# Causal attention and a cosine MoE in one kernel: tail scores of two pairs together, one transpose for both tails, P V a step later

## The chip, the cores and the metric

The kernel runs on one core of one Trainium2 chip. The metric is device time in microseconds, the median of several runs. The clock that TensorE (PE) was granted stood at 1.00 of its full 2.4 GHz in every stage of the profiled execution.

## What is computed

```python
scores = (1 / sqrt(64)) * q @ k^T          # 4 batches, 12 heads, 448 tokens, head size 64
scores = where(causal mask, -1e9, scores)
attn   = softmax(scores)
x      = (attn @ v) with the heads side by side          # 1792 x 768
h      = x @ w_in                                        # w_in 768 x 2048
out    = (h * cos(h)) @ w_out                            # w_out 2048 x 768
```

Everything is float32.

## The kernel before, in words

The program has an attention stage and a MoE stage. All of it is written out by hand: inside `tc.manual_schedule()` each engine runs its instructions in the order in which the code issues them, so the place of a line in `attention` (L219) is its place in the queue of PE, DVE (VectorE), ACT (ScalarE), POOL (GpSimd) or SP (the queue of loads and stores).

**Attention.** A *pair* is two heads of one batch; there are 24. The 448 tokens are three blocks of 128 and a *tail* of 64. Step `i` of the loop starts pair `i` and carries on with pairs `i-1` to `i-3`:

- PE forms the scores of pair `i`: blocks of 128 rows in `scores_main` (L349, L354; first the *top* block of 384 columns for both heads, then the *low* blocks of 128 and 256), and the tail's 64 rows for both heads in `scores_tail` (L361, L364). Head 0 lies on partitions 0 to 63 of the operands and head 1 on 64 to 127, so that the two heads' products use different rows of the array. In the tail the outputs lie on different partitions of one PSUM bank too.
- PE turns Q and K of pair `i+1`: three blocks each (L319) and one 64-row tail each (L326).
- ACT copies both to SBUF (`evac_qk`, L336 and L338).
- DVE adds the mask, negates and takes the row minimum (`masked`, L372); ACT takes the exponential and the row sum (`exp`, L386); DVE inverts the sums (L397, L398); POOL multiplies (`normalise`, L404).
- PE turns the weights of pair `i-1`: twelve blocks (`tp_blocks`, L426) and the tail as four (`tp_tail`, L436). DVE copies two of the four banks out (L555, L557) and ACT two (L564, L566).
- PE multiplies by V for pair `i-2` (`av`, L450). ACT and DVE write the result as a high and a low part (L466, L470) in the next step.

PSUM has eight banks. `new_bank` hands out 0 to 3 in turn and `score_bank` 4 to 7: the scores of step `i` go into the banks that the turned weights of step `i-1` left.

After each step half of a weight piece is converted (`convert_weight`, L126): even halves take two DVE operations (L134, L137) and a square on ACT (L140), odd halves two DVE operations (L143, L147), a copy on ACT (L148) and a subtraction on POOL (L149). There are twelve pieces, so 24 steps have one half each.

After the last pair, two steps have 18 matmuls of the first MoE product each in front of the turned weights (`fill`, L476).

**MoE.** Slots of two token blocks by eight feature groups (`slot`, L875) follow, and then a stage with fewer products for the remaining tokens (from L1027 on). Only slot `k == 3` is touched, by the order in which its DVE, ACT and POOL work is issued: `c1` are the cosine's stages (L593 to L600), `pb` the packing of a raw weight (L168, L172, L176), `halve` its split into high and low (L702, L703), `m2a_chunk` the products L681 and their sum on DVE (L669).

Of the kernel before, what the change touches and what calls it, by code (L numbers as in the profile page):

```python
# [21 lines left out]
def kernel(  # L22
# [68 lines left out]
    def new_bank():  # L91
        return banks8[:, bank("p", 0, 1, 2, 3)]

    packed = banks8[:, 2:4, 0:EH]

    def score_bank():
        return banks8[:, bank("s", 4, 5, 6, 7)]
# [28 lines left out]
    def convert_weight(st, w, pool, parts=1, j=0, halves=(0, 1)):  # L126
# [4 lines left out]
        if 0 in halves:  # L131
# [8 lines left out]
            nc.scalar.activation(hif, hif, AF.Square)  # L140
        if 1 in halves:
# [6 lines left out]
            nc.scalar.copy(wh, tf)  # L148
# [70 lines left out]
    def attention(filler):  # L219
        with (  # L220
# [3 lines left out]
            rows = f32(land.rearrange("p a e u -> p (a e u)")).rearrange(  # L224
                "p (t c d) -> p t c d", c=NB + 1, d=P
            )
            qn_t = [rows[:, i] for i in range(3)]
            kn_t = [rows[:, 3 + i] for i in range(3)]
            vn_t = [cst.tile([P, NB + 1, P], F32, name=f"vn{i}") for i in range(4)]
# [3 lines left out]
            nat, qkt, prob, ptr = {}, {}, {}, {}  # L233
# [4 lines left out]
            def load_main(dst, src, b, h0, eng=nc.sync):  # L238
                for j in range(2):
                    eng.dma_start(  # L240
                        out=dst[:, 0:NB, heads(j)],
                        in_=src[b, h0 + j, 0 : NB * P, :].rearrange("(c p) d -> p c d", p=P),
                    )

            def load_tail(dst, src, b, h0, eng=nc.sync, p=0):
                eng.dma_start(
                    out=dst[p : p + TAIL, NB, :].rearrange("p (h d) -> p h d", h=2),
                    in_=src[b, h0 : h0 + 2, NB * P : S, :].rearrange("h p d -> p h d"),
                )

            def load_qk(i, keng=nc.sync):
                b, hp = pairs[i]
                qn = qn_t[i % 3]
                kn = kn_t[i % 3]
                load_main(qn, q, b, 2 * hp)
                load_main(kn, k, b, 2 * hp, keng)
                load_tail(qn, q, b, 2 * hp)
                load_tail(qn, k, b, 2 * hp, keng, TAIL)
                nat[i] = [qn, kn]
# [3 lines left out]

            for i in range(3):
                if i == 0:
                    load_qk(0, nc.scalar)

                    nc.scalar.copy(cst.tile([P, 32], BF16, name="tab")[:, 0:1], warm[:, 0:1])
                elif i == 1:
                    load_qk(1, nc.scalar)  # L270
            wps = new_bank()

            def keep_warm(n):
                for _ in range(n):
                    nc.tensor.matmul(wps[:, 0:P], lhsT=warm, rhs=warm, start=True, stop=True)
# [1139 lines left out]
```

## Time and profile before

| | us |
|---|---|
| median of 3 runs (632.76 to 634.29) | 632.78 |
| the profiled execution | 632.72 |
| its span | 630.9 |
| attention, steps 0 to 2 | 17.98 |
| attention, steps 3 to 22 | 143.73 |
| attention, step 23 to the start of the MoE slots | 20.82 |
| PE busy | 622.0 (99%) |
| DVE, ACT, POOL busy | 485.8, 431.5, 438.5 |

A row of the chain names the work that the end of the program waited for at each moment. A timeline row gives start, duration, engine, line, operation and shapes, and in brackets the idle time before it with what ended it. PE's float32 products stand as two records each, one for each pass, and operations that run at once on different rows or columns of the array overlap. Between operations of one engine the difference of two starts says what one costs; a duration includes the tail that the next one overlaps. `128x448` is partitions by columns.

### The profile page before, as it was taken

The page shows a single profiled execution, that of the slowest core. Times are in us where ns is not written, and L with a number is a line of the kernel's source. Part 1 is how long each engine was busy: PE and PEld are TensorE (multiplying, and loading weights), DVE is VectorE, ACT ScalarE, POOL GpSimd, SP SyncE. Part 2 cuts the span into 40 slices and gives each one's busy share as a digit, 9 for nine tenths or more (in the row PEclk, how much of TensorE's full clock was granted, in tenths as well). Part 3 has the DMA queues.
Part 4 walks back from the last instruction along what each step waited for, and adds up shares of the span by engine and source line. Part 5 has one row for each costly group of instructions (what it writes and reads, how often), then busy time and mean ns, then how long its engine had stood idle before and what let it go on. Part 6 is the DMA issues. An engine that isn't in the chain of part 4 may idle for free.

```text
span 630.9 us, 11559 instructions
## 1 busy us (share of the span) xinstructions
PE 622.0 (99%) x3753; PEld 536.2 (85%) x3753; DVE 485.8 (77%) x1072; ACT 431.5 (68%) x953; POOL 438.5 (69%) x432
## 2 busy tenths in 40 slices
PE   9999999999999999999999999999999999999996
PEld 6666666666679998899999999999999999999996
DVE  6988888888847778877777777774358877887887
ACT  5998999999877677877787777753346545644640
POOL 3656656566534868887877778781578789788886
PEclk9999999999999999999999999999999999999999
DMA  6656546456403676969796969769997477559204
GB/s 148 153 133 164 132 114 157 114 139 175 126 10 118 226 280 225 352 223 325 228 341 199 337 224 313 250 235 360 400 403 279 151 258 253 178 170 316 86 2 150
DMA packets 124620, 133.28 MB, mean 211 GB/s; under 512 B 72688, under 2 KB 108896, under 8 KB 124560
## 3 DMA queue, kind: packets, MB, share of 16 engines
q1 hardware_dynamic: 116944, 106.23, 53.2%
q0 software_dynamic: 4928, 24.78, 10.6%
q10 hardware_dynamic: 2688, 1.54, 0.8%
q8 instruction: 30, 0.49, 0.3%
q14 instruction: 30, 0.25, 0.1%
HBM read 82.58 MB, written 49.94 MB: 210 GB/s over the span
## 4 chain that ended last, share of the span: by engine, by line
PE 91%; DVE 4%; ACT 2%; issue 1%; POOL 1%; DVEq 0%
PE banks L681 18%; PE banks L1103 12%; PE banks L1123 12%; PE banks L450 7%; PE banks L585 6%; PE banks L586 6%; PE banks L587 6%; PE banks L354 5%; PE banks L426 5%; PE banks L319 4%; PE banks L364 3%; PE banks L1027 2%; PE banks L1140 2%; PE banks L436 2%; PE banks L326 1%
## 5 line engine op out<-in xcount | busy, mean ns | idle before, releaser
L669 DVE TENSOR_TENSOR acc<-acc,banks 128x768 f32<-128x768 f32 (+1 forms) x122 | 112.7, 932 | 43.8 <-PE banks L681 33.5
L681 PE MATMUL banks<-w,gh 128*128 128x384 f32 x512 | 109.7, 335 | 1.6 <-DVE acc L669 1.6
L404 POOL TENSOR_TENSOR pb<-pb,stat 128x768 f32<-128x768 f32 (+2 forms) x72 | 74.0, 1042 | 50.4 <-ACT pb L386 35.4
L681 PEld LDWEIGHTS banks<-w,gh 128*128 128x128 f32 x512 | 90.8, 188 | 3.2 <-DVE acc L669 2.0
L386 ACT ACTIVATE pb<-pb,stat 128x384 f32<-128x384 f32 (+1 forms) x144 | 71.9, 504 | 9.4 <-DVE stat L372 9.4
L585 PE MATMUL banks<-xa,w 128*128 128x512 f32 x192 | 75.1, 391 | 0.0
L587 PE MATMUL banks<-xa,w 128*128 128x512 f32 x192 | 75.0, 391 | 0.0
L586 PE MATMUL banks<-xa,w 128*128 128x512 f32 x192 | 75.0, 391 | 0.0
L372 DVE CUSTOM_DVE_ANT_0 pb<-banks,mask 128x384 f32<-128x384 f32 (+1 forms) x144 | 53.2, 419 | 17.2 <-PE banks L354 9.2
L681 PE MATMUL banks<-w,gl 128*128 128x384 f32 x256 | 65.1, 335 | 0.0
L703 POOL TENSOR_TENSOR w<-ct,w 128x768 fp32r<-128x768 f32 x28 | 52.0, 1857 | 17.7 <-ACT w L702 12.5
L593 ACT ACTIVATE ni<-banks 128x512 int32<-128x512 f32 (+1 forms) x64 | 34.5, 539 | 33.9 <-PE banks L587 20.0
L612 POOL TENSOR_TENSOR gl<-r,gh 128x512 fp32r<-128x512 f32 x32 | 41.6, 1301 | 19.4 <-ACT gh L611 19.2
L595 DVE SCALAR_TENSOR_TENSOR r<-ni,banks 128x512 f32<-128x512 int32 (+1 forms) x56 | 35.1, 626 | 20.2 <-ACT ni L593 16.9
L597 ACT ACTIVATE r<-r 128x512 f32<-128x512 f32 (+1 forms) x56 | 32.8, 586 | 23.3 <-DVE r L595 22.8
L450 PE MATMUL banks<-pm,vn 128*64 128x448 f32 (+3 forms) x384 | 46.8, 386 | 0.0
L681 PEld LDWEIGHTS banks<-w,gl 128*128 128x128 f32 x256 | 46.4, 188 | 0.0
L1103 PE MATMUL banks<-xb,bb 128*128 128x384 f32 x234 | 44.7, 334 | 0.0
L600 DVE SCALAR_TENSOR_TENSOR r<-r,banks 128x512 f32<-128x512 f32 (+1 forms) x56 | 35.1, 626 | 12.2 <-ACT r L598 12.2
L450 PEld LDWEIGHTS banks<-pm,vn 128*64 128x64 f32 x384 | 25.4, 136 | 22.3 <-issue 15.4
L1123 PE MATMUL banks<-big,gh 128*128 128x384 f32 x168 | 42.6, 334 | 0.0
L587 PEld LDWEIGHTS banks<-xa,w 128*128 128x128 f32 x192 | 36.0, 188 | 7.6
(151 smaller groups left out, 1559.1 us busy)
## 6 DMA issues: line engine op xcount, KB each, us to landing
bb<-w_in_d SPq DMA_DIRECT2D x48, 384.0 KB, 5.4
land<-in_moe_w_in_dram SPq DMA_DIRECT2D x14, 768.0 KB, 5.3
land<-in_moe_w_out_dram SPq DMA_DIRECT2D x14, 768.0 KB, 5.5
w_out_d<-w POOLq DMA_DIRECT2D x14, 768.0 KB, 5.2
big<-w_out_d SPq DMA_DIRECT2D x25, 384.0 KB, 5.2
w_in_d<-w POOLq DMA_DIRECT2D x7, 768.0 KB, 3.9
raw_d<-ct POOLq DMA_DIRECT2D x14, 384.0 KB, 7.2
land<-in_q_dram SPq DMA_DIRECT2D x48, 96.0 KB, 2.8
```

Of the source, the lines that this page charges most:

```text
L372: nc.vector.tensor_tensor_reduce(out=dst, in0=src, in1=m, scale=-1.0, scalar=3.0e38, op0=ALU.add, op1=ALU.min, accum_out=st[:, 0, n : n + 1],)
L386: nc.scalar.activation(dst, dst, AF.Exp, scale=-1.0, bias=st[:, 0, n : n + 1], accum_out=st[:, 1, n : n + 1],)
L404: nc.gpsimd.tensor_tensor(dst, dst, r.to_broadcast(list(dst.shape)), op=ALU.mult)
L450: nc.tensor.matmul(o[heads(j), kc * P : S], lhsT=vn[:, kc, heads(j)], rhs=pm[:, kc, j, kc * P : S], start=(kc == 0), stop=(kc == NB),)
L585: yield nc.tensor.matmul(hv, lhsT=wh[:, f], rhs=x[:, 0, cc, t], start=(cc == 0), stop=False)
L586: yield nc.tensor.matmul(hv, lhsT=wh[:, f], rhs=x[:, 1, cc, t], start=False, stop=False)
L587: yield nc.tensor.matmul(hv, lhsT=wl[:, f], rhs=x[:, 0, cc, t], start=False, stop=(cc == NCC - 1))
L669: nc.vector.tensor_tensor(d, d, o, op=ALU.subtract)
L681: nc.tensor.matmul(o[:, e, 0:EH], lhsT=a[:, cs], rhs=w[:, e * EH : (e + 1) * EH], start=(x == 0), stop=(x == 5),)
L703: nc.gpsimd.tensor_tensor(w[:, 1], tf, f32(w[:, 0]), op=ALU.subtract)
L1103: nc.tensor.matmul(o, lhsT=w[:, u, k * P : (k + 1) * P], rhs=x[k][:, v], start=k + m == 0, stop=k == K - 1 and m == 2,)
L1123: nc.tensor.matmul(o[:, b % 2, 0:EH], lhsT=g_ops[i][u][:, c * P : (c + 1) * P], rhs=wouts[g, i][:, v], start=(x == 0), stop=(x == 2),)
```

## The change

1. **Tail scores.** `scores_tail` goes. In odd steps `scores_ends(i - 1)` forms the tails of pairs `i-1` and `i` together: 384 key columns for two pairs and two heads (four products of 64 rows by 64 columns of the array), then the last 64 key columns for the four. The odd pair's heads are swapped on the output side (`j ^ p % 2`), which puts the four on the four quarters of the array, and the two pairs have a bank each (2 and 3).
2. **One transpose for both tails.** The tails of Q and K are loaded one above the other and turned by one 128x128 transpose (`transpose_ends`) into 128 columns behind Q. Tails of two pairs are loaded by one transfer. Q is copied out as 512 columns and K as 384, without the factor 1/8, which goes into `masked`.
3. **A step later.** The tail's mask, exponential, normalising and transposes trail by a step, P V is for pair `i-3`, and `pm` has three buffers. The loop has one step more, V is loaded a step later, and the filler is cut 14, 12, 10 instead of 18, 18.
4. **Banks by hand.** 0 is P V's, 1 takes Q and later K of the next pair, 4 to 7 the scores and then the turned weights; K's transposes move behind those of the weights.
5. **Weights.** The square (L140) and the copy (L148) go from ACT to POOL.
6. **MoE slot 3.** `pb` and `halve` are issued ahead of the last stages of `c1`.

```diff
-            nc.scalar.activation(hif, hif, AF.Square)
+            nc.gpsimd.tensor_tensor(hif, hif, hif, op=ALU.mult)
...
+            nc.gpsimd.tensor_copy(wh, tf)
             nc.gpsimd.tensor_tensor(wl, tf, f32(wh), op=ALU.subtract)
...
+            def transpose_main(i, which, b):
+                t = qkt[i, which] = flat[:, 2 * which + i % 2], banks8[:, b]
                 for c in range(NB):
+                    nc.tensor.transpose(t[1][:, c * P : (c + 1) * P], nat[i][which][:, c, :], ident)
+
+            def transpose_ends(i, b):
+                nc.tensor.transpose(banks8[:, b, W : W + P], nat[i][2], ident)
...
+            def scores_ends(i):
+
+                for r, w in ((0, W), (W, P // 2)):
+                    for p in (i, i + 1):
+                        qt, kt = qkt[p, 0][0], qkt[p, 1][0]
+                        for j in range(2):
+                            nc.tensor.matmul(
+                                banks8[heads(j ^ p % 2), (TA_BANK, TB_BANK)[p % 2], r : r + w],
+                                lhsT=qt[heads(j), W:S],
+                                rhs=(kt[heads(j), 0:W] if r == 0 else qt[heads(j), S : S + P // 2]),
+                                start=(r == 0), stop=(r != 0),
+                            )
...
-                    out=dst, in0=src, in1=m, scale=-1.0, scalar=3.0e38,
+                    out=dst, in0=src, in1=m, scale=-scale, scalar=3.0e38,
...
-                ptr[i] = at.tile([P, 2 * JUMP], F32, tag="pm", bufs=2, name="pm")
+                ptr[i] = at.tile([P, 2, LEN], F32, tag="pm", bufs=3, name="pm")
...
             def fill(n):
-                for _ in zip(range(n), filler):
+                if not extra:
+                    spare = itertools.cycle((QK, 6))
+                    extra.append(filler_of(lambda: banks8[:, next(spare)]))
+                for _ in zip(range(n), extra[0]):
                     pass
...
+            for i in range(N + 4):
                 cur, prev, nxt = i < N, 0 < i <= N, i + 1 < N
-                old, done = 0 <= i - 2 < N, 0 <= i - 3 < N
+                ends_of, old, done = 0 <= i - 2 < N, 0 <= i - 3 < N, 0 <= i - 4 < N
+                tb = (4, (TA_BANK, 6)[i % 2], 5, (6, 7)[i % 2])
...
-                    load_v(i)
+                if prev:
+                    load_v(i - 1)
...
                 if cur:
                     open_scores(i)
-                    pb, pl, st = prob[i]
-                    top = scores_main(i, TOP)
-                    low = scores_main(i, LOW)
...
-                    tail = scores_tail(i)
-                if nxt and i:
-                    transpose_qk(i + 1, 0)
-                    transpose_tails(i + 1)
-                    transpose_qk(i + 1, 1)
+                    scores_main(i, TOP, SC[0:2])
+                    scores_main(i, LOW, SC[2:4])
+                    if i % 2:
+                        scores_ends(i - 1)
...
+                elif nxt:
+                    transpose_main(i + 1, 0, QK)
+                    transpose_ends(i + 1, QK)
                 if done:
-                    finish_hi(i - 3, av_of[i - 3])
+                    finish_hi(i - 4)
...
+                if 0 < i <= N + 1:
+                    inverse(i - 1, 0 if prev else TAIL_COL, TAIL_COL + (i > 1))
...
-                    inverse(i - 1, LO)
                     normalise_block(i - 1, 0)
                     normalise_block(i - 1, 1)
...
-                if prev:
-                    inverse(i - 1, TL)
-                    normalise(prob[i - 1][1][:, 0:S], prob[i - 1][2], TL)
+                if ends_of:
+                    normalise_ends(i - 2)
...
                         exp_block(i, 2, j)
+                        if i and nxt and j == i % 2:
+                            evac_qk(i + 1, 0, n=W + P)
...
-                    finish_lo(i - 3, av_of.pop(i - 3))
+                    finish_lo(i - 4)
...
+                    inverse(i, TOP_COL, TOP_COL + 2)
+                    normalise_block(i, 2)
+                    masked_block(i, 0, 1, 0, SC[3])
+                    masked_block(i, 1, 1, P, SC[3])
+                    exp_block(i, 0, 0)
+                    exp_block(i, 1, 0)
+                if prev:
+                    masked_ends(i - 1)
+                if i in (N, N + 1):
+                    fill((14, 12)[i - N])
+                if prev:
+                    open_ptr(i - 1)
+                    tp_top(i - 1, tb[0])
+                    tp_first(i - 1, tb[1])
+                if prev:
+                    tp_last(i - 1, tb[2])
                 if nxt and i:
-                    evac_qk(i + 1, 0)
+                    transpose_main(i + 1, 1, QK)
                     evac_qk(i + 1, 1)
                 if cur:
...
+                    exp_block(i, 0, 1)
+                    exp_block(i, 1, 1)
...
+                    exp_ends(i - 1)
+                if ends_of:
+                    tp_ends(i - 2, tb[3])
+                    evac_ends(i - 2, tb[3])
+                if i == N + 2:
+                    run(extra[0])
                 if old:
-                    av_of[i - 2] = av(i - 2)
-                if i == N + 1:
-                    run(filler)
+                    av(i - 3)
...
-                    some(c1)
-                    some(pb)
-                    some(c1)
-                    m2a_chunk(*prev, 1)
-                    run(pb)
-                    tb = halve(ib)
+                    if k == 2:
+                        some(c1)
+                        some(pb)
+                        some(c1)
+                        m2a_chunk(*prev, 1)
+                        run(pb)
+                        tb = halve(ib)
+                    else:
+                        run(pb)
+                        m2a_chunk(*prev, 1)
+                        tb = halve(ib)
+                        some(c1, 2)
```

The order on PE, where a step is what lies between two groups of scores (`pb`, `pl`: the weights' main part and tail; `pm`: turned; `land`: Q and K as loaded). A step before:

```order
L354 MATMUL banks<-flat 128x384 x2
L354 MATMUL banks<-flat 128x128 x2
L354 MATMUL banks<-flat 128x256 x2
L364 MATMUL banks<-flat 64x448 x2
L319 MATMUL banks<-ident,land 128x128 x3
L326 MATMUL banks<-ident,land 128x64 x2
L319 MATMUL banks<-ident,land 128x128 x3
L426 MATMUL banks<-ident,pb 128x128 x12
L436 MATMUL banks<-ident,pl_92 128x128 x4
L450 MATMUL banks<-pm,vn_89 64x448 x2
```

And an odd step of the change; an even one is the same without the two rows of L348:

```order
L336 MATMUL banks<-flat 128x384 x2
L336 MATMUL banks<-flat 128x128 x2
L336 MATMUL banks<-flat 128x256 x2
L348 MATMUL banks<-flat 64x384 x4
L348 MATMUL banks<-flat 64x64 x4
L304 MATMUL banks<-ident,land 128x128 x3
L307 MATMUL banks<-ident,land 128x128
L422 MATMUL banks<-ident,pb 128x128 x12
L304 MATMUL banks<-ident,land 128x128 x3
L442 MATMUL banks<-ident,pl_95 128x128 x4
L457 MATMUL banks<-pm,vn_88 64x448 x2
```

The 23 transposes of a step now stand in one row, and the tail's products come in every second step.

ACT in the same place, an even step of the change (L376 is `exp`, L313 any copy out of PSUM, L475 the high part of P V):

```order
L475 CAST xa<-banks 128x448
L376 ACTIVATE pb,stat<-pb,stat 128x384
L313 COPY flat<-banks 128x512
L376 ACTIVATE pb,stat<-pb,stat 128x384
L376 ACTIVATE pb,stat<-pb,stat 128x128
L376 ACTIVATE pb,stat<-pb,stat 128x256
L313 COPY pm<-banks 128x2x2x128
L313 COPY flat<-banks 128x384
L376 ACTIVATE pb,stat<-pb,stat 128x128
L376 ACTIVATE pb,stat<-pb,stat 128x256
L376 ACTIVATE pl_95,stat<-pl_95,stat 128x448
L313 COPY pm<-banks 128x4x2x64
```

Before, the last copy out of the turned weights stood ahead of three exponentials; now it is the last of the step, and no weight work stands in the queue.

POOL across an odd and an even step of the change (L396 is `normalise`, L134 the square, L142 the copy, L143 the subtraction):

```order
L134 TENSOR_TENSOR st<-st 128x256
L396 TENSOR_TENSOR pb<-pb,stat 128x2x128
L396 TENSOR_TENSOR pb<-pb,stat 128x2x256
L396 TENSOR_TENSOR pl_94<-pl_94,stat 128x448
L396 TENSOR_TENSOR pb<-pb,stat 128x2x384
L142 CAST w_287<-ct 128x256
L143 TENSOR_TENSOR w_287<-ct,w_287 128x256
L396 TENSOR_TENSOR pb<-pb,stat 128x2x128
```

The square and the copy now stand ahead of the next step's first two multiplications.

## Rows read from the trace of the kernel before

**Rows 1.** page, part 1: busy time of each engine over the whole span.

```profile
PE 622.0 (99%) x3753; PEld 536.2 (85%) x3753; DVE 485.8 (77%) x1072; ACT 431.5 (68%) x953; POOL 438.5 (69%) x432
```

**Rows 2.** busy time by stage; columns: window, us, PE, PEld, DVE, ACT, POOL, PEclk, DMA, GB/s.

```profile
6.72:24.70 17.98, 17.26 (x124) 10.83 (x124) 16.42 (x66) 15.68 (x53) 9.41 (x9) 1.00 0.63 148
24.70:168.43 143.73, 143.73 (x1122) 93.37 (x1122) 125.63 (x506) 131.03 (x407) 86.77 (x90) 1.00 0.56 137
168.43:189.25 20.82, 20.52 (x133) 14.40 (x133) 11.13 (x37) 16.08 (x36) 8.08 (x10) 1.00 0.21 62
```

**Rows 3.** chain that ended last, one step; columns: start us, us, what.

```profile
60.63 1.50 PE banks L354 x12
62.13 0.90 PE banks L364 x4
63.03 0.48 PE banks L319 x3
63.51 0.21 PE banks L326 x2
63.71 0.48 PE banks L319 x3
64.19 1.31 PE banks L426 x12
65.50 0.44 PE banks L436 x4
65.94 1.88 PE banks L450 x16
```

**Rows 4.** tail products by line L364, window 54.8:55.0, then 53.3:60.8; min/median/max ns.

```profile
L364 PE MATMUL banks<-flat x2: 587/587/587, 54.9 to 54.9; 64*64 64x448 f32 x2
...
L364 PE MATMUL banks<-flat x4: 536/562/587, 54.9 to 55.3; 64*64 64x448 f32 x4
```

**Rows 5.** timeline of ACT, the step from 60.63; columns: start us, us, instruction.

```profile
62.27 0.61 ACT L386 ACTIVATE pb<-pb,stat 128x384 f32<-128x384 f32 x1 [0.48 <-DVE stat L372]
...
64.67 0.39 ACT L386 ACTIVATE pb<-pb,stat 128x128 f32<-128x128 f32 x1
...
65.05 0.39 ACT L386 ACTIVATE pb<-pb,stat 128x128 f32<-128x128 f32 x1
...
65.53 0.59 ACT L564 COPY pm<-banks 128x512 f32<-128x512 f32 x1
66.02 0.59 ACT L566 COPY pm<-banks 128x512 f32<-128x512 f32 x1
66.50 0.52 ACT L386 ACTIVATE pb<-pb,stat 128x256 f32<-128x256 f32 x1
...
67.00 0.50 ACT L386 ACTIVATE pb<-pb,stat 128x256 f32<-128x256 f32 x1
...
67.49 0.66 ACT L386 ACTIVATE pl<-pl,stat 128x448 f32<-128x448 f32 x1
```

**Rows 6.** groups by form of two steps, POOL; count, busy us, mean ns, idle before.

```profile
L404 POOL TENSOR_TENSOR pb<-pb,stat 128x512 f32<-128x512 f32 x2 | 2.1, 1043 | 0.0
...
L404 POOL TENSOR_TENSOR pb<-pb,stat 128x256 f32<-128x256 f32 x2 | 1.2, 615 | 1.1 <-DVE stat L398 1.1
...
L149 POOL TENSOR_TENSOR w<-ct,w 128x256 fp32r<-128x256 f32 x1 | 0.7, 728 | 1.6 <-ACT w L148 1.6
```

**Rows 7.** chain that ended last, end of the attention stage.

```profile
175.10 0.43 PE banks L585
...
179.44 1.31 PE banks L426 x12
```

**Rows 8.** timeline of PE, then of DVE, around the MoE stage's one PE wait.

```profile
253.15 0.97 PE L681 MATMUL banks<-w,gh 128*128 128x384 f32 x4 [1.64 <-DVE acc L669]
...
252.15 1.81 DVE L669 TENSOR_TENSOR acc<-acc,banks 128x768 f32<-128x768 f32 x2
```

**Rows 9.** page, part 6: loads of Q; KB each, median us to landing.

```profile
land<-in_q_dram SPq DMA_DIRECT2D x48, 96.0 KB, 2.8
```

More of the change, by code (lines that the diff above doesn't have):

```diff
@@ L213, with attention @@
     PARTS = 3
-    def attention(filler):
+    def attention(filler_of):
         with (
@@ L223, in attention @@
         ):
[L224 to L229, printed above, removed]
+            rows = f32(land.rearrange("p a e u -> p (a e u)"))
+            W = NB * P
+            main_t = rows[:, 0 : 6 * W].rearrange("p (t c d) -> p t c d", c=NB, d=P)
+            qn_t = [main_t[:, i] for i in range(3)]
+            kn_t = [main_t[:, 3 + i] for i in range(3)]
+            ends = [rows[:, 6 * W + i * 2 * P : 6 * W + (i + 1) * 2 * P] for i in range(3)]
+            vn_t = [cst.tile([P, NB, P], F32, name=f"vn{i}") for i in range(4)]
+            vt_t = [cst.tile([P, 2 * P], F32, name=f"vt{i}") for i in range(2)]
             pl_t = [cst.tile([P, (NB + 1) * P], F32, name=f"pl{i}") for i in range(2)]
@@ L352, in scores_main, with open_stat, col @@
+            def open_stat(i):
+                stats[i] = at.tile([P, 3, 8], F32, tag="stat", bufs=3, name="stat")
+            def col(c, j):
+                return (0, 2, TOP_COL)[c] + j
+            def scores_main(i, blocks, banks):
+                qt, kt = qkt[i, 0][0], qkt[i, 1][0]
                 for c, o, w in blocks:
@@ L450, in av @@
                         nc.tensor.matmul(
-                            o[heads(j), kc * P : S], lhsT=vn[:, kc, heads(j)],
-                            rhs=pm[:, kc, j, kc * P : S], start=(kc == 0), stop=(kc == NB),
+                            o[heads(j), kc * P : S],
+                            lhsT=(vn[:, kc] if kc < NB else vt)[:, heads(j)],
+                            rhs=ptr[i][:, j ^ i % 2, kc * (KS + P) : kc * KS + S],
+                            start=(kc == 0), stop=(kc == NB),
                         )
@@ L521, in attention @@
                     normalise_block(i - 1, 1)
-                if cur and i != 1:
-                    for j in range(2):
-                        masked_block(i, top, 2, j, 0)
-                if prev:
-                    inverse(i - 1, TL)
-                    normalise(prob[i - 1][1][:, 0:S], prob[i - 1][2], TL)
+                if ends_of:
+                    normalise_ends(i - 2)
                 if cur:
                     for j in range(2):
+                        if i != 1:
+                            masked_block(i, 2, j, 0, SC[j])
@@ L1350 @@
         raw_out = []
-        for i in attention(filler):
+        for i in attention(filler_of):
             while raw_out:
```

300 lines of the change are left out of this document (123 added, 177 removed).

## The prediction

> **What bounds the kernel now.** I read the busy shares first: PE is busy for 99% of the span and no other engine above 77% [rows 1]. Then the stages: in the 20 attention steps from 24.70 to 168.43 PE is never idle, while ACT is busy 131.03 and DVE 125.63 of 143.73 us [rows 2]. One step is 143.73/20 = 7.187 us, and the chain of one step is PE alone, piece after piece [rows 3]. So there PE work that goes away is time that goes away, until the next engine is reached. That is near: ACT needs 131.03/20 = 6.55 us a step and DVE 6.28. The rest of the program is PE as well, with one wait of 1.64 us in the MoE slots [rows 8]; the change touches nothing after them. The granted clock is 1.00 in all three stages [rows 2], and I leave it there. The profiled execution took 632.72 us, 1.8 more than its span; the median of the runs is 632.78. All sums are made against 632.72. About 0.3% (1.9 us) is what a measurement can tell from no change.
>
> **PE work per step.** P V streams 448 + 320 + 192 + 64 = 1024 columns in two passes, the two heads at once, in 1.88 us [rows 3]. About 0.15 of that is the change of shape: three transposes take 0.48 where twelve in a row take 1.31, 0.109 each, so 0.48 - 0.33 = 0.15 goes to the start and the end of a group [rows 3]. A column of one pass then costs (1.88 - 0.15)/2048 = 0.845 ns.
> - Tails today: 0.90 a step [rows 3], which is two passes of 448 columns (0.76) and 0.15. That the heads run at once is seen in the two records that start together at 54.9 and last 587 ns each; four records of 562 ns fit in under 1 us [rows 4].
> - Tails after: if the four products of a round run at once, two passes of 384 columns (0.65), two of 64 (0.11) and 0.15, so 0.90 again, but in every second step only. No row shows four at once. Bounds: 0.90, and 1.65 to 1.72 if they go two by two (another 0.75, and half a start). I take four at once: heads on different rows already run together [rows 4], and so do heads on different columns in P V [rows 3].
> - Transposes: today 0.48 + 0.21 + 0.48 for Q, tails and K, and 1.31 + 0.44 for the weights, 2.92 in all [rows 3]. After: 23 in a row, 23 x 0.109 + 0.15 = 2.66.
> - Scores (1.50) and P V (1.88) stay.
>
> An even step is 1.50 + 2.66 + 1.88 = 6.04 and an odd one 6.94: 12.98 for two, against 14.37. By PE alone that is 1.39 less, 13.9 over the ten double steps.
>
> **What is late next.** ACT loses the square and the copy, but has now the last copy of a step (the turned tails, into the bank that the next step's low scores want) at the very end of its queue. An even step, from its start on PE: ACT's first exponential starts after 1.64 (62.27 against 60.63) [rows 3, 5]. Then, by the differences of starts in [rows 5] and the duration where there is none: 384 columns 0.61, Q's copy of 512 0.48, 384 columns 0.61, 128 columns 0.38, 256 columns 0.50, copy of 512 0.48, K's copy 0.42 (between the 128-column exponential and the 512-column copy, 0.38 and 0.49), 0.38, 0.49, the tail's exponential 0.66, the last copy 0.59. Together 5.60, so it ends at 7.24. PE wants that bank after its own 6.04 and the top scores, half of 1.50: at 6.79. It waits 0.45. In an odd step Q's copy waits for the transposes behind the tail products (1.50 + 0.90 + 0.05 + 0.44 + 0.16 = 3.05) and ACT ends at 3.05 + 0.48 + 3.90 = 7.43, while PE comes at 6.94 + 0.45 + 0.75 = 8.14: no wait. So a double step is 13.43, 0.945 less than now, and the 20 steps give **-9.45**. Bounds: -13.9 (no wait) and -5 (ACT 0.45 slower again per double step).
>
> DVE loses a pair of small operations a step and is below 6.28; it has 6.7 on the mean. POOL is busy 86.77/20 = 4.34 a step [rows 2] and gets the square or the copy. Neither stands in the trace on POOL; the nearest rows are 256 columns with two inputs, 0.615 and 0.728, and 512 columns, 1.043 [rows 6]. I take 0.7 for the square and 0.5 for the copy, which has one input; bounds 0.3 and 1.3. The copy is the one that counts: behind it stand the subtraction 0.73 and the two multiplications 0.57 and 1.04, which feed the second group of turned weights. With DVE done some 0.3 after the step's start they end near 0.3 + 0.5 + 0.73 + 0.57 + 1.04 = 3.1. PE reaches that group in an odd step after 1.50 + 0.45 + 0.90 + 0.05 + 8 x 0.109 = 3.8. So 0.7 of cover, and no cost.
>
> **Start.** Steps 0 to 2 take 17.98 with DVE busy 16.42 and ACT 15.68 [rows 2]; PE would lose 3 x 0.70 and one P V (1.88), 4.0. Those engines keep nearly all their work, so I take **-1.0**, bounds 0 and -4.0.
>
> **End.** From step 23 on it takes 20.82 now [rows 2]. After: step 23 is 1.50 + 0.45 + 0.90 + 16 transposes (1.90 with the change of shape) + 1.88 = 6.63; three more P V 5.64; 20 transposes, of which 16 in step 24 and 4 in step 25, 2.48 with their changes; 36 filler matmuls at 4.34 for 18 [rows 7], 8.7, and 0.3 for being cut in three. Sum 23.75, so **+2.9**: P V and the tails, a step later, are paid here. Bounds +2.4 (no wait) and +4.
>
> **MoE slot 3.** The wait of 1.64 ends with DVE's sum [rows 8], and DVE, ACT and POOL hand work to each other all the way back into slot 3. The new order starts `halve` about one DVE operation of 0.9 earlier and the next raw load 1.4 earlier, and the cosine later by as much. I take **-0.6**; bounds -1.64 and +0.5.
>
> **No price:** loads. SP has 6 a step and 3 more every second one instead of 9; they land in 2.8 us [rows 9], and V is needed two steps after its load. DVE's masking has a factor -1/8 where it had -1: same operation and shapes.
>
> Sum: -9.45 - 1.0 + 2.9 - 0.6 = -8.15; 632.72 - 8.15 = **624.6 us**.
>
> **Rivals.**
> 1. *ACT keeps up.* Its exponentials start 0.03 to 0.05 earlier in some steps and the copies are short; without the wait the steps give -13.9 and the end +2.4: 632.72 - 13.9 - 1.0 + 2.4 - 0.6 = 619.6. For it: ACT's sum falls to some 6.1 a step against 6.49 on the mean. Against: the order above, which leaves the last copy no room in an even step.
> 2. *Two by two.* The four products take turns in pairs, because each bank gets two of them from different rows of the array. Each of the twelve blocks then costs 0.75 to 0.9 more: 624.6 + 12 x 0.82 = 634.4, slower than before. It decides once a block takes more than about 0.90 + 8.15/12 = 1.58. Against it: today's tail already writes one bank from both halves of the rows at once [rows 4]. The Trainium skill, page "TensorEngine Tiling (Array Packing)", section "Restrictions and Gotchas", says that different row tiles cannot access the same PSUM bank simultaneously. By that rule each pair's two heads would exclude each other and the result would be this rival's 634.4 or worse; the trace, with two records of 587 ns starting together, does not agree for outputs on different partitions.
> 3. *POOL is late.* If the copy takes 1.3 or more, or DVE is later, the second group waits: 0.3 every second step, 12 x 0.3 = 3.6, so 628.2. It decides when the copy exceeds 0.5 + 0.7 = 1.2.
>
> **How the numbers follow.** Forecast 0.58 (its own range 621.5 to 627.0, from the bounds of the start, the end and slot 3), ACT keeps up 0.14, two by two 0.13, POOL late 0.11, anything else 0.04. The range 619.5 to 629.0 takes in all but two by two and the rest, 0.17. Faster by over 0.3% is below 630.8: the forecast, rivals 1 and 3 and a little more, 0.85. Rival 2 lies on the border of 634.6 and is shared: same 0.08, slower 0.07.
>
> **What would show it.** Steps that alternate near 6.04 and 7.4; a tail block of some 0.90 with eight records of 384 columns, four starting together; one row of 23 transposes; a PE wait of about 0.45 ahead of the low scores of odd steps, ended by ACT's copy. The square and copy on POOL below 1.2. The end stage 23 to 24 us long, and the wait in the MoE slots shorter than 1.64. I am wrong if the four do not start together, if another wait stands in every step, or if the end grows by more than 4.

## The result, and the profile after

The changed kernel took **627.28 us** (median of 4 runs, 626.94 to 627.49), the kernel before 632.77 beside it: a ratio of 0.9909 with a 95% interval from 0.9891 to 0.9926. Measured again later, it took 626.47 (625.40 to 627.54), a ratio of 0.9900 (0.9883 to 0.9916). Forecast: 624.6, range 619.5 to 629.0. The profiled execution took 627.32, its span is 625.5.

Part 1 of the page after, the line that answers to [rows 1]: PE has lost 12 us of work, but the span only 5.4. In steps 3 to 22 PE is now idle for 2.92 us (135.66 - 132.74 in the second row below), where it was never idle before.

```profile
PE 609.8 (97%) x3825; PEld 537.2 (86%) x3825; DVE 476.1 (76%) x1023; ACT 419.5 (67%) x928; POOL 449.3 (72%) x456
```

The same three stages as in [rows 2], cut where steps 0, 3 and 23 and the MoE slots begin in the kernel after (columns as there):

```profile
6.92:23.07 16.15, 12.17 (x103) 8.71 (x103) 12.23 (x57) 13.03 (x45) 9.10 (x9) 1.00 0.77 179
23.07:158.73 135.66, 132.74 (x1181) 94.53 (x1181) 117.99 (x466) 120.34 (x388) 96.07 (x110) 1.00 0.58 142
158.73:183.34 24.61, 23.66 (x168) 16.11 (x164) 13.84 (x42) 19.38 (x42) 11.41 (x14) 1.00 0.22 60
```

With the start of the last product (625.65 before, 619.12 after) the whole span can be accounted for. Both kernels are divided here at starts of PE's timeline. The later bounds of [rows 2] are starts of the chain, some 0.07 after these, so its first stage is 17.90 by this measure:

| part, us | before | after | difference | predicted |
|---|---|---|---|---|
| up to the first scores | 6.72 | 6.92 | +0.20 | 0 |
| steps 0 to 2 | 17.90 | 16.15 | -1.75 | -1.0 |
| steps 3 to 22 | 143.73 | 135.66 | -8.07 | -9.45 |
| step 23 to the MoE slots | 20.83 | 24.61 | +3.78 | +2.9 |
| slots to the last product | 436.47 | 435.78 | -0.69 | -0.6 |
| last product to the end | 5.29 | 6.42 | +1.13 | 0 |
| sum | 630.94 | 625.54 | -5.40 | -8.15 |

The timeline of PE after shows an odd step (from 131.64), an even one (from 139.14) and the last P V. L336 are the scores, L348 the tail products, L304 and L307 the transposes of Q, K and their tails, L422 and L442 those of the weights and their tails, L457 is P V:

```profile
131.64 0.92 PE L336 MATMUL banks<-flat 64*128 64x384 f32 x4
132.83 0.93 PE L336 MATMUL banks<-flat 64*128 64x128 f32 x8 [0.27 <-ACT pm L313]
133.68 0.99 PE L348 MATMUL banks<-flat 64*64 64x384 f32 x16
134.60 0.55 PE L304 MATMUL banks<-ident,land 128*128 128x128 f32 x3
...
135.09 1.47 PE L422 MATMUL banks<-ident,pb 128*128 128x128 f32 x12
...
136.73 0.60 PE L442 MATMUL banks<-ident,pl 128*128 128x128 f32 x4
137.26 1.84 PE L457 MATMUL banks<-pm,vn 128*64 128x448 f32 x12
...
139.14 1.57 PE L336 MATMUL banks<-flat 64*128 64x384 f32 x12
140.64 0.55 PE L304 MATMUL banks<-ident,land 128*128 128x128 f32 x3
...
145.19 0.59 PE L336 MATMUL banks<-flat 64*128 64x384 f32 x2
...
181.47 1.84 PE L457 MATMUL banks<-pm,vn 128*64 128x448 f32 x12 [0.66 <-DVE xb L479]
```

The odd step takes 139.14 - 131.64 = 7.50, the even one 6.05 (6.04 in most). In the even step the scores take 140.64 - 139.14 = 1.50. In the odd one they take 133.68 - 131.64 = 2.04, and the bracket names what the low scores wait for: ACT's copy `pm`, L313, which ends at 132.78. The brackets count from the modelled end of the records before; the difference of starts, **0.54**, is the whole cost. The tail block takes 134.60 - 133.68 = 0.92. That copy on ACT, and POOL's multiplications of the two low blocks in the same step:

```profile
132.21 0.57 ACT L313 COPY pm<-banks 128x512 f32<-128x512 f32 x1
...
133.82 1.62 POOL L396 TENSOR_TENSOR pb<-pb,stat 128x256 f32<-128x256 f32 x2
```

The view of L348 by itself, in 0.3 us around such a block, shows its first four products with one start (to 0.1 us; the four starts lie within 0.02 in the block of 133.68):

```profile
L348 PE MATMUL banks<-flat x4: 533/533/533, 160.8 to 160.8; 64*64 64x384 f32 x4
```

PE's waits over the whole span (what waited and for what; us in total, times, longest):

```profile
PE banks L336 <- ACT pm L313: 3.2, 11, 0.5
...
PE banks L685 <- DVE acc L673: 0.6, 2, 0.4
```

POOL in one double step, by form (count, busy us, mean ns, idle before): the square, L134, takes 0.61, the copy, L142, 0.40.

```profile
L134 POOL TENSOR_TENSOR st<-st 128x256 f32<-128x256 f32 x1 | 0.6, 614 | 0.9 <-DVE ct L131 0.9
L142 POOL CAST w<-ct 128x256 fp32r<-128x256 f32 x1 | 0.4, 398 | 1.6 <-DVE ct L141 1.6
```

### The profile page after: what moved, and what is told of

Its sections match the earlier page's. It is cut to its first block, busy times and chain, and to the rows that moved or that the text cites. A ratio compares the mean times of both kernels' runs of the same rounds, so it can differ in the third digit from the quotient of the medians.

```text
span 625.5 us, 11531 instructions
## 1 busy us (share of the span) xinstructions
PE 609.8 (97%) x3825; PEld 537.2 (86%) x3825; DVE 476.1 (76%) x1023; ACT 419.5 (67%) x928; POOL 449.3 (72%) x456
## 4 chain that ended last, share of the span: by engine, by line
PE 59%; DVE 2%; ACT 1%; issue 0%; DVEq 0%; ACTq 0%
PE banks L685 17%; PE banks L1113 12%; PE banks L1133 12%; PE banks L590 5%; PE banks L591 5%; PE banks L589 5%; PE banks L1037 2%; PE banks L1150 2%; DVE ct L170 0%; DVE acc L1160 0%; DVE banks L166 0%; DVE banks L162 0%; DVE r L599 0%; DVE acc L673 0%; DVE sct L770 0%
## 5 line engine op out<-in xcount | busy, mean ns | idle before, releaser
L685 PE MATMUL banks<-w,gh 128*128 128x384 f32 x512 | 109.8, 335 | 0.6 <-DVE acc L673 0.6
L685 PEld LDWEIGHTS banks<-w,gh 128*128 128x128 f32 x512 | 90.8, 188 | 2.4 <-DVE acc L673 1.3
L396 POOL TENSOR_TENSOR pb<-pb,stat 128x768 f32<-128x768 f32 (+2 forms) x72 | 74.0, 1042 | 24.9 <-DVE stat L390 10.1
L376 ACT ACTIVATE pb<-pb,stat 128x384 f32<-128x384 f32 (+1 forms) x144 | 72.1, 504 | 13.4 <-DVE stat L357 13.4
L685 PE MATMUL banks<-w,gl 128*128 128x384 f32 x256 | 65.1, 335 | 0.0
L357 DVE CUSTOM_DVE_ANT_0 pb<-banks,mask 128x384 f32<-128x384 f32 (+1 forms) x144 | 53.9, 418 | 7.9 <-PE banks L336 7.6
L336 PE MATMUL banks<-flat 64*128 64x256 f32 (+2 forms) x288 | 40.7, 402 | 6.2 <-ACT pm L313 3.2
L685 PEld LDWEIGHTS banks<-w,gl 128*128 128x128 f32 x256 | 46.4, 188 | 0.0
L604 DVE SCALAR_TENSOR_TENSOR r<-r,banks 128x512 f32<-128x512 f32 (+1 forms) x56 | 35.1, 626 | 14.0 <-ACT r L602 13.9
L457 PE MATMUL banks<-pm,vn 128*64 128x192 f32 (+2 forms) x288 | 44.1, 441 | 0.7 <-DVE xb L479 0.7
```

Source lines behind the costliest of these rows:

```text
L357: nc.vector.tensor_tensor_reduce(out=dst, in0=src, in1=m, scale=-scale, scalar=3.0e38, op0=ALU.add, op1=ALU.min, accum_out=st[:, 0, n : n ...
L376: nc.scalar.activation(dst, dst, AF.Exp, scale=-1.0, bias=st[:, 0, n : n + 1], accum_out=st[:, 1, n : n + 1],)
L396: nc.gpsimd.tensor_tensor(dst, dst, r.to_broadcast(list(dst.shape)), op=ALU.mult)
L457: nc.tensor.matmul(o[heads(j), kc * P : S], lhsT=(vn[:, kc] if kc < NB else vt)[:, heads(j)], rhs=ptr[i][:, j ^ i % 2, kc * (KS + P) : kc ...
L685: nc.tensor.matmul(o[:, e, 0:EH], lhsT=a[:, cs], rhs=w[:, e * EH : (e + 1) * EH], start=(x == 0), stop=(x == 5),)
```

## The experiments

All are edits of the changed kernel. Step times are differences of starts in the trace; times are medians, ratios are to the kernel before.

| kernel | even, odd step | last product | us | ratio (95%) |
|---|---|---|---|---|
| changed, repeated | 6.04, 7.51 | 618.97 | 626.47 | 0.9900 (0.9883 to 0.9916) |
| two_by_two | 6.04, 8.25 | 628.23 | 634.11 | 1.0018 (1.0010 to 1.0026) |
| ends_first | 6.04, 8.03 | 624.74 | 632.07 | 0.9989 (0.9981 to 0.9998) |
| act_weights | 6.04, 7.56 | 620.15 | 627.37 | 0.9911 (0.9898 to 0.9923) |
| early_copy | 6.18, 7.15 | 617.11 | 624.46 | 0.9872 (0.9857 to 0.9887) |
| slot_before | 6.04, 7.51 | 619.74 | 628.02 | 0.9923 (0.9909 to 0.9937) |
| av_bank | 6.04, 7.51 | 625.06 | 630.99 | 0.9968 (0.9955 to 0.9981) |
| av_bank7 | 6.04, 7.50 | 618.79 | 625.91 | 0.9892 (0.9875 to 0.9908) |
| early_split_late | 6.04, 7.25 | 616.66 | 623.15 | 0.9849 (0.9832 to 0.9865) |
| best | 6.54, 6.96 | 617.72 | 624.73 | 0.9874 (0.9859 to 0.9889) |
| best_av7 | 6.54, 6.96 | 617.15 | 623.77 | 0.9859 (0.9844 to 0.9874) |
| **all_orders** | 6.04, 6.96 | 611.50 | **618.51** | 0.9775 (0.9761 to 0.9789) |

### Do the four products run at once? (two_by_two)

```diff
-  banks8[heads(j ^ p % 2), (TA_BANK, TB_BANK)[p % 2], r : r + w],
+  banks8[heads(j), (TA_BANK, TB_BANK)[p % 2], r : r + w],
```

The swap of the odd pair's heads is taken out behind it too (`tp_blocks`, `av`).

> The four tail products of two pairs are put on two quarters of the array instead of four (the odd pair uses the quarters of the even one), nothing else changes. Theory (all four run together, block of four 384-column records 0.37 and second round 0.32, 0.90 in all): each of the 12 blocks now runs its first round twice and its second twice, 1.65 instead of 0.90, so odd steps become 7.50 + 0.75 = 8.25 and the time 627.3 + 12 x 0.75 = 636.3 (635 to 638). Rival (the four only start together in the records, and products that share a bank run one after the other anyway): no change, 627.3 within 0.7, block still 0.90 to 1.0.

The timeline of PE, the rows that answer to those above:

```profile
138.22 0.92 PE L336 MATMUL banks<-flat 64*128 64x384 f32 x4
...
140.25 1.74 PE L348 MATMUL banks<-flat 64*64 64x384 f32 x16
141.92 0.55 PE L304 MATMUL banks<-ident,land 128*128 128x128 f32 x3
...
146.46 1.57 PE L336 MATMUL banks<-flat 64*128 64x384 f32 x12
```

The block takes 141.92 - 140.25 = 1.67 and the odd step 8.24. That is the 0.75 that was priced. Steps 3 to 22 take 143.12 instead of the repeated changed kernel's 135.75, but the blocks of steps 1 and 23 lengthen their stages by only 0.25 each, so the twelve together cost 7.9 and not 9. That fits the median, which rose by 7.6 to 634.11, just short of the 635 to 638 expected. The last product comes 9.3 later, since two more things differ there: the first scores start 0.6 later, and one wait in the MoE stage, in code that is the same, is longer by 0.7. So four products at once are real, and with them taken away the change is worth nothing (1.0018). By the rule that the prediction cited from the Trainium skill ("TensorEngine Tiling (Array Packing)", "Restrictions and Gotchas": different row tiles cannot access the same PSUM bank simultaneously) the two heads of a pair would have taken turns in both kernels; the trace does not agree, 0.92 against 1.67.

### What stands behind the bank wait? (early_copy, ends_first, act_weights)

```diff
-                if prev:
-                    exp_ends(i - 1)
                 if ends_of:
                     tp_ends(i - 2, tb[3])
                     evac_ends(i - 2, tb[3])
+                if prev:
+                    exp_ends(i - 1)
```

> ACT copies the transposed tails out of their bank before the exp of the new tails instead of after it: the copy that the odd step's low scores wait for ends 0.75 earlier, the exp of the tails 0.46 later. Theory A (only the bank): odd steps 7.50 -> 6.96, time 621.4 (620.5 to 622.5). Theory B (the chain exp of the tails, merged inverse on DVE, normalising on POOL, transposes is as long): what the odd step gains the even step or the transposes lose, double step 13.54 -> 13.2 to 13.5, time 624 to 627.3.

The wait for ACT's copy is gone from the steps, but the double step fell by 0.21 only, not by 0.54. The timeline shows PE's block transposes in an even and an odd step, 1.61 and 1.66 long where they were 1.47:

```profile
139.22 1.61 PE L422 MATMUL banks<-ident,pb 128*128 128x128 f32 x12
...
146.32 1.66 PE L422 MATMUL banks<-ident,pb 128*128 128x128 f32 x12
```

and POOL's normalising of the two low blocks, L396, which feeds them:

```profile
138.29 1.61 POOL L396 TENSOR_TENSOR pb<-pb,stat 128x256 f32<-128x256 f32 x2 [0.65 <-ACT xb L475]
...
145.45 1.61 POOL L396 TENSOR_TENSOR pb<-pb,stat 128x256 f32<-128x256 f32 x2
```

In the odd step it ends at 147.06. Four transposes of the top block come first, and those of the block that is normalised last would start six transposes in, at 146.32 + 6 x 0.109 = 146.97. The two stretches, 0.14 and 0.19, are all that even (6.18) and odd (7.15) steps have above 6.04 and 6.96. Theory B holds: POOL stands right behind the bank.

```diff
                     scores_main(i, TOP, SC[0:2])
-                    scores_main(i, LOW, SC[2:4])
                     if i % 2:
                         scores_ends(i - 1)
+                    scores_main(i, LOW, SC[2:4])
```

> In odd steps the tail block (0.90) is issued between the top scores and the low scores, so PE comes to the low scores 0.90 later and ACT's copy out of their bank (0.54 late now) is done. Theory A (this bank wait alone makes the odd step longer than PE's work): odd steps 7.50 -> 6.96, time 627.3 - 11 x 0.54 = 621.4 (620.5 to 622.5). Theory B (POOL's normalising of the low blocks, which ends about 162.5 in the step from 158.73 and for which the transposes of that step already stretch from 1.47 to 1.76, stands right behind the bank wait): the wait moves to the transposes, odd steps 7.30 to 7.50, time 625 to 627.6, and the PE row of the block transposes takes over 1.9 in odd steps.

Neither theory holds. The kernel became slower by 5.6 us, and odd steps took 8.03. PE waits for the bank no more, but for another thing, ahead of the tails' transposes:

```profile
139.86 0.49 PE L304 MATMUL banks<-ident,land 128*128 128x128 f32 x3
140.90 0.63 PE L442 MATMUL banks<-ident,pl 128*128 128x128 f32 x4 [0.55 <-DVE stat L357]
```

In odd steps these go to bank 7, the second low bank, whose masks (L357) stand on DVE behind the inverse of the top sums, L389. DVE:

```profile
139.30 0.72 DVE L389 TENSOR_SCALAR stat<-stat 128x2 f32<-128x2 f32 x1
...
140.32 0.42 DVE L357 CUSTOM_DVE_ANT_0 pb<-banks,mask 128x256 f32<-128x256 f32 x1
```

POOL at that time:

```profile
139.05 0.93 POOL L396 TENSOR_TENSOR pl<-pl,stat 128x448 f32<-128x448 f32 x1
```

An operation on two columns took 0.72, where the same takes 0.17 elsewhere, and ended at 140.02, just after POOL's multiplication (139.98). In the changed kernel the same inverse takes 0.40 and ends just after POOL's low blocks (133.82 + 1.62 = 135.44). So the low scores, 0.9 later, put DVE's short inverse under the next POOL instruction, and the masks, the bank and PE were late after it. The Trainium skill, "SBUF — State Buffer", section "SBUF: two separate sides", says that GpSimd shares a pair of SBUF ports with DVE operations in a two-port mode or with two SBUF inputs, and that whichever starts first holds the pair for its whole instruction. The trace agrees for this inverse, with 0.72 against 0.17; in which mode it ran no run shows.

```diff
-            nc.gpsimd.tensor_tensor(hif, hif, hif, op=ALU.mult)
+            nc.scalar.activation(hif, hif, AF.Square)
...
-            nc.gpsimd.tensor_copy(wh, tf)
+            nc.scalar.copy(wh, tf)
```

> The 12 squares (0.61 on POOL) and 12 copies (0.40 on POOL) of the weights go back to ACT (about 0.3 each), all else stays changed. Theory 1 (both engines are off the path at these places): 627.3 within 0.7. Theory 2 (ACT is what the odd step waits for, so POOL saved 0.3 in each of 24 steps): 627.3 + 7 = 634. Theory 3 (POOL's late normalising is the bound behind the bank wait): POOL comes to the normalising 0.2 to 0.4 earlier in odd steps, the transposes of odd steps shrink from 1.76 to 1.47, time 624 to 626.5.

Theory 1 comes nearest: 627.37, against 627.28 and 626.47 of the changed kernel. The profile does show a small price. Odd steps take 7.56 instead of 7.51, and the stage from step 23 to the slots 25.01 instead of 24.66, some 0.8 in all. So this part of the change, the weights' square and copy on POOL, is worth less than 1 us while the bank sets the pace.

### The end, and the third slot (av_bank, av_bank7, slot_before, after_again)

```diff
+            def o_bank(i):
+                return 4 if i == N - 1 else O
...
-                o = banks8[:, O]
+                o = banks8[:, o_bank(i)]
```

`finish_hi` and `finish_lo` read from the same bank.

> P V of the last pair goes to bank 4, which is free by then, and need not wait until DVE has read the pair before out of bank 0 (0.66 us of PE at 181.47). Theory: PE's wait is gone and the stage from step 23 to the slots takes 24.6 - 0.66 = 23.9, time 627.3 - 0.6 = 626.7. Rival (the products behind it wait for the same DVE and ACT work instead): 24.4 to 24.7, no change in the time.

Neither the theory nor the rival holds. PE's wait of 0.66 ahead of the last P V went, and one of 3.32 came behind it: the first slot's product wants bank 4, which DVE has not yet read. The choice of bank was bad. PE:

```profile
183.47 0.28 PE L460 MATMUL banks<-pm,vt 128*64 128x64 f32 x4
187.08 0.50 PE L592 MATMUL banks<-xa,w 128*128 128x512 f32 x1 [3.32 <-DVE xb L482]
```

Its busy time by stretch (window, us, PE busy, granted clock, DMA share, GB/s) shows that the wait cost more than itself:

```profile
188.00:189.00 1.00, 1.00 (x5) 0.71 0.00 0
189.00:190.00 1.00, 1.00 (x4) 0.50 0.00 0
...
191.00:192.00 1.00, 1.00 (x5) 0.59 0.00 0
```

Some 1.3 us after PE began again, the granted clock fell from 2.4 to 1.2 GHz, for 3.4 us. The same happened in this run in step 3, behind waits of 1.26 and 0.49, and made that step 9.29 long instead of 7.72. Such waits do not bring it about each time: the changed kernel has the same two in step 3, and its clock stood at 1.00 there. The profiled execution (632.54) is also the slowest of the twelve, which begin at 628.81, so the median of 630.99 holds less of this.

With bank 7 (`return 7`), which no product wants so early:

> As with bank 4, but P V of the last pair goes to bank 7, which no product wants before the first pair of output banks at about 191.6, so the slots' first product (banks 4 and 5) has nothing to wait for. Theory: the wait of 0.66 at 181.47 goes and nothing takes its place; from step 23 to the slots 24.6 - 0.66 = 23.9, last product 0.6 earlier than in the changed kernel's two profiles (619.0), time 626.5 - 0.6 = 625.9. Rival (DVE and ACT, late with the last pairs, make the slot's first products or their cosines wait): last product within 0.2 of 619.0, time 626.5.

```profile
180.47 0.39 PE L594 MATMUL banks<-xa,w 128*128 128x512 f32 x1
180.78 1.84 PE L460 MATMUL banks<-pm,vn 128*64 128x448 f32 x12
...
182.66 0.50 PE L592 MATMUL banks<-xa,w 128*128 128x512 f32 x1
```

P V follows without a wait. From step 23 (158.79) to the slots it takes 23.87 instead of 24.66, and the time is 625.91 against 626.47: the place is shown by the trace, while the intervals of the two times overlap.

```diff
-                    if k == 2:
                         some(c1)
                         some(pb)
                         some(c1)
                         m2a_chunk(*prev, 1)
                         run(pb)
                         tb = halve(ib)
-                    else:
-                        run(pb)
-                        m2a_chunk(*prev, 1)
-                        tb = halve(ib)
-                        some(c1, 2)
```

> The third slot of the mixture of experts emits its operations in the order of before, all else stays changed. Theory (the new order takes about 1 us off PE's wait of 1.64 in that slot): the wait is 1.6 again and the last product is 0.7 to 1.0 later against the changed kernel, time 628.0 to 628.3. Rival (the wait went for another reason, the order is worth nothing): last product within 0.2, time 627.3.

With the old order the wait is back:

```profile
246.62 0.97 PE L685 MATMUL banks<-w,gh 128*128 128x384 f32 x4 [1.56 <-DVE acc L673]
...
468.24 0.97 PE L1127 MATMUL banks<-big 128*128 128x384 f32 x4 [0.32 <-DVE acc L671]
```

Both profiles of the changed kernel show waits of 0.6 to 0.7 in all at L685. From the slots' start to the last product it takes 437.01, in the repeated changed kernel 435.76, which is 1.25 more. Only 0.65 of that has arisen 150 us after the slots' start, and this is the order's worth. The other 0.60 arises at the second wait, some 220 us behind slot 3, in code that the edit does not touch; the same place is longer by 0.3 to 0.7 in three kernels that have the new order (act_weights, av_bank7, two_by_two).

> The changed kernel unaltered, for the 1.1 us more than before that lay behind its last product (6.42 us from the last product's start to the end of the span, before 5.29; four other kernels with the same end took 4.85 to 5.19). Theory X (the last transfer happened to be slower there): again the last product at about 619.1, but 4.8 to 5.3 us behind it, time 625.9 to 626.5. Theory Y (it belongs to the changed kernel): 6.4 us again, time 627.3.

Theory X: 5.35 behind the last product and 624.32 in all in the profiled execution. Over all kernels of the study with the same end this stretch lay between 4.84 and 6.42, so the 1.1 us of the first profile cannot be put down to the change, and a single profile of this program can be off by that much.

### A better order (early_split_late, best, best_av7, all_orders)

early_split_late changes three orders. The first is the early copy. The second takes the inverse of the tails apart, as shown here. The third, not shown, puts POOL's `tensor_copy` and subtraction of the weights into `run_later`, called behind `normalise_block(i, 2)`:

```diff
-                if 0 < i <= N + 1:
-                    inverse(i - 1, 0 if prev else TAIL_COL, TAIL_COL + (i > 1))
+                if prev:
+                    inverse(i - 1, 0, TAIL_COL)
...
+                if ends_of:
+                    inverse(i - 1, TAIL_COL, TAIL_COL + 1)
+                    normalise_ends(i - 2)
```

> Three orders at once: ACT's copy out of the low scores' bank ahead of the exp of the tails; the inverse of the tails apart from that of the low blocks, so that the latter does not wait for the exp of the tails; POOL's copy and subtraction of the weights behind the normalising of the step, not ahead of it. Theory B (behind the bank wait stands the chain DVE inverse, POOL normalising, transposes, with POOL's weight work in it): no wait is left, steps 6.04 and 6.96 (double step 13.00, with the early copy alone 13.33, changed kernel 13.54), time 624.5 - 11 x 0.33 = 620.9, with the shorter third step 620 to 621.5. Rival (DVE or ACT is full, or POOL's work in its new place collides with the normalising of the top blocks): double step 13.2 to 13.4, time 623.5 to 624.6.

The odd step went to 7.25 only, so the double step of 13.29 falls in the rival's range. PE:

```profile
133.65 0.49 PE L311 MATMUL banks<-ident,land 128*128 128x128 f32 x3
134.24 0.63 PE L449 MATMUL banks<-ident,pl 128*128 128x128 f32 x4
```

The tails' transposes could start 0.33 after the three of K, at 133.98, and start 0.26 later. DVE (L396 is the inverse, L364 the mask here):

```profile
131.58 0.15 DVE L396 TENSOR_SCALAR stat<-stat 128x1 f32<-128x1 f32 x1
...
132.98 0.37 DVE L396 TENSOR_SCALAR stat<-stat 128x2 f32<-128x2 f32 x1
...
133.66 0.42 DVE L364 CUSTOM_DVE_ANT_0 pb<-banks,mask 128x256 f32<-128x256 f32 x1
```

POOL at that time:

```profile
130.82 1.61 POOL L403 TENSOR_TENSOR pb<-pb,stat 128x256 f32<-128x256 f32 x2 [1.95 <-DVE stat L397]
132.39 0.94 POOL L403 TENSOR_TENSOR pl<-pl,stat 128x448 f32<-128x448 f32 x1
```

It is the wait of ends_first again: an inverse that lasts until POOL's multiplication (132.39 + 0.94 = 133.33) is done, and behind it the mask for bank 7. The tails' inverse, on one column only, is not held: it takes 0.15 in the middle of POOL's low blocks.

In best the masks of the second low bank go ahead of that inverse, and the tails' inverse behind the masks of the first low bank:

```diff
-                    inverse(i, TOP_COL, TOP_COL + 2)
-                    normalise_block(i, 2)
                     masked_block(i, 0, 1, 0, SC[3])
                     masked_block(i, 1, 1, P, SC[3])
+                    inverse(i, TOP_COL, TOP_COL + 2)
+                    normalise_block(i, 2)
```

> The three orders of the run before (early copy, inverse of the tails apart, POOL's weight copy and subtraction last), and on DVE the masks of the second low bank ahead of the inverse of the top blocks, the inverse of the tails behind the masks of the first low bank. Theory (in odd steps the transposes of the tails waited 0.56 for bank 7, whose mask stood behind an inverse that was held 0.43 instead of 0.17 until POOL's normalising ended): odd steps 7.25 -> 6.95 to 7.05, even steps 6.04 to 6.15, double step 13.0 to 13.15, time 623.15 - 11 x 0.25 = 620.4 (619.5 to 621.5). Rival (the later inverse makes POOL's normalising of the top blocks and the next transposes late): double step 13.25 or more, time 623 or more.

Odd steps are at 6.96, as expected, but even steps went to 6.54: the double step of 13.50 and the time of 624.73 are the rival's. POOL starts the tails' normalising late, after the late inverse:

```profile
154.38 0.93 POOL L403 TENSOR_TENSOR pl<-pl,stat 128x448 f32<-128x448 f32 x1 [0.38 <-DVE stat L397]
```

and PE's transposes of the tails start at 155.37, where 154.76 + 0.33 = 155.09 was possible. Those 0.28 are about half of the 0.50; another 0.17 is in the block transposes ahead of them, which take 1.64 instead of 1.47.

> The kernel before in this call, with P V of the last pair in bank 7. If both gains stand: 0.4 to 0.7 less than that kernel, 619.8 (619 to 621). If the end stage gives the wait back elsewhere: the same time as that kernel.

The stage from step 23 to the slots fell from 23.98 to 23.24, the last product came 0.57 earlier than in best and the time was lower by 0.96: both gains stand. The 619.8 named as the result rested on the time expected of best, which was missed.

all_orders starts from best_av7. The tails' inverse is back ahead of the low masks, and `run_later`, which now has the square too, is called behind `normalise_ends(i - 2)`.

> Early copy, inverse of the tails apart and ahead of the low masks again, masks of the second low bank ahead of the inverse of the top blocks, P V of the last pair in bank 7, and both of POOL's weight jobs (square; copy and subtraction) between the normalising of the tails and that of the top blocks. Theory (what made even steps 6.54 in the kernel named best was the tails' normalising, late behind POOL's square and the late inverse; what made odd steps 7.25 in early_split_late was the mask behind the held inverse; both go here): even steps 6.04 to 6.1, odd steps 6.96 to 7.05, double step 13.0 to 13.15 against 13.29 and 13.50, time 623.15 - 11 x 0.2 - 0.6 = 620.3 (619.5 to 621.3). Rival (POOL's and DVE's work of a step is too tightly linked: what one gets earlier the other gets later): double step 13.3 or more, time 622.5 or more.

PE, and the line of part 1 of the page:

```profile
133.01 1.57 PE L346 MATMUL banks<-flat 64*128 64x384 f32 x12
...
139.05 1.57 PE L346 MATMUL banks<-flat 64*128 64x384 f32 x12
...
146.01 1.57 PE L346 MATMUL banks<-flat 64*128 64x384 f32 x12
```

```profile
PE 606.2 (98%) x3825; PEld 536.1 (87%) x3825; DVE 479.0 (78%) x1069; ACT 420.4 (68%) x928; POOL 449.0 (73%) x456
```

Even steps take 6.04, odd ones 6.96: what PE's own work takes. The time is below the 619.5 to 621.3 expected: against early_split_late the profile has 2.7 less in steps 3 to 22, 0.6 less in steps 0 to 2 and 1.5 less from step 23 to the slots. With 618.51 this kernel is 2.25% faster than the one before and 8.0 us faster than the changed one.

## Why the prediction was right, and where it was not

- **The mechanism.** A tail block of 0.92 in every second step (predicted 0.90), even steps of 6.04 (6.04), a wait for ACT's copy into the low scores' bank in every odd step. PE's prices were right to a few hundredths. Rival 2, priced at 0.82 a block, cost 0.75 where it was built.
- **The sum.** That 627.28 and 626.47 came so near to 624.6 is in part luck, since the start gave 0.75 more than forecast while the steps gave 1.38 less and the end cost 0.9 more. The narrower range given for the forecast alone, 621.5 to 627.0, holds only the second of the two.
- **Steps, -9.45; measured -8.07.** The mis-sized term is the wait: 0.45 was predicted and 0.54 found. ACT's copy ended about when it was expected to; but the low scores, once released, also took 0.85 (133.68 - 132.83) instead of the 0.75 that they take without a wait in all_orders. That is 0.1 in each of ten odd steps. The tail block's 0.92 adds 0.02 to each, and another 0.2 is step 3, which took 7.72 and not 7.50.
- **The bounds of that term.** "ACT keeps up" would have given 13.9. early_copy shows that this rival had left something out: without the wait steps 3 to 22 take 133.91, another 1.8 less, not 5.8, because POOL stands behind the bank. Rival 3 named the place, the second group of turned weights, but as what happens if POOL's copy is slow. The copy took 0.40, and POOL was late all the same: the prediction let it finish 3.1 after the start of an odd step, while its two multiplications end at 3.80 (133.82 + 1.62 - 131.64). The cover of 0.7 was nearly used up before anything went wrong.
- **Start, -1.0; measured -1.75**, within its bounds. The third step fell from 7.69 to 6.61. The runs show what it hangs on without settling all of it: it took 5.95 with the tails' inverse apart and 5.40 in all_orders, so it is DVE's and POOL's order, not their amount of work, that sets it. The prediction had reasoned from the amount.
- **End, +2.9; measured +3.78**, with 24.61 just beyond the 23 to 24 named as a sign. The part that was missed is the 0.66 that P V of the last pair waits for the only P V bank; av_bank7 took it away and got 0.8 back.
- **MoE slot 3, -0.6; measured -0.69.** The size was right, and slot_before confirms it: the order itself is worth 0.65.
- **Behind the last product** the first profile had 1.13 more, and the same kernel had 5.35 there in after_again, nearly the 5.29 of before. The two measurements put the change at 5.5 us (0.9909) and 6.2 us (0.9900), with intervals that overlap, against 8.15 predicted.

## What to carry to other kernels

When PE gives up work, find for every step the second and the third wait behind the first one, with their ends in us, before pricing the gain: here three of them (ACT's copy, POOL's normalising, DVE's mask) lay within 0.6 us, and getting round the first alone gave 0.2 of 0.54 or even cost 0.5. The cure was order, not less work: each engine's queue was sorted so that what PE waits for comes first, and short DVE operations do not fall under a long POOL one. Before giving a late result a bank of its own, look who wants that bank next.

## What was not expected of the hardware

- Two products on different rows of the array, with outputs on different partitions of one PSUM bank, run at once, and so do four on the four quarters with two banks: 0.92 against 1.67 us for the block.
- DVE's addition on 128x2 elements in SBUF took 0.17 us alone. When it began under a POOL instruction it never ended first: it ended 0.02 to 0.10 us behind POOL's in all 198 cases of these traces, after up to 0.88 us. The same addition on 128x1 took 0.15 at most and ended up to 0.77 us before POOL's did.
- In av_bank, after PE had waited for 3.32 us, the granted clock fell to 1.2 GHz some 1.3 us after PE had resumed and stayed there for 3.4 us. In step 3 it fell there after waits that left it at 2.4 GHz in the changed kernel.
- The stretch from the last product to the end of the span, the same code in all kernels here, took 4.84 to 6.42 us.
